# Chunked attention with two feed-forward layers: a new opening and other tiles for four split jobs

## The chip, the cores and the metric

The program runs on one core of one Trainium2 chip. The metric is the device time of one execution in microseconds (us).

## The reference

Attention over chunks of 32 queries, each with 8 memory keys and the 56 keys around the chunk, then two feed-forward layers over 3072 tokens. All is float32.

```python
for c in range(nc):                                    # 24 chunks, (B, H, S, D) = (4, 8, 768, 64)
    k_full = np.concatenate([mem_k, k_ctx], axis=2)    # 8 + 16 + 32 + 8 keys
    scores = scale * np.matmul(q_c, k_full.transpose(0, 1, 3, 2))
    a = np.exp(scores - np.max(scores, axis=-1, keepdims=True))
    out[:, :, c_start:c_end] = np.matmul(a / (np.sum(a, axis=-1, keepdims=True) + 1e-09), v_full)
x = out.transpose(0, 2, 1, 3).reshape(B * S, H * D)    # 3072 x 512
h = x @ w_in                                           # layer 1: 512 -> 2048
x = (np.maximum(h, 0.0) + np.log1p(np.exp(-np.abs(h)))) @ w_out
h = x @ moe2_w_in                                      # layer 2
return (h - np.tanh(h)) @ moe2_w_out
```

## The kernel before

**Products.** Every operand of the layers is split into a rounded high part and a low rest, and each product is three products on TensorE (`mm3`: high·high, high·low, low·high). The weights arrive as 64-bit words, and ScalarE and VectorE turn them into the two parts (`split_w`).

**Layout of the work.** The tokens are 24 attention units of 128 and six blocks of 512 tokens. An **opening** computes units 0 to 3 (tokens of block 0), splits the sixteen weight pairs of layer 1 and runs layer 1 on block 0. A main loop runs layer 1 on blocks 1 to 3, with the other attention units and jobs of the next layer stepped in between by `tick`. Then come one layer-1 phase (`y_phase`) and, for three groups of 1024 tokens, layer 2 as `h_phase` and `y_phase`. From the fourth block on the layers use seven block products instead of eight (`PRODUCTS`), for which `job_x` makes sums and differences of the layer-1 result `y1d`, splits each of them and stores it as `x2d`.

**What sets the order.** On TensorE, VectorE, ScalarE and SyncE (SP) instructions stand in the order of the code, and an engine that waits holds up all that is behind. In the opening a list of tokens, `OPENING`, is that order. For an attention unit u: Su scores, mxu maximum, exu exponentials, mlu normalization, Tu transposes, pTu their copy, Vu product with the values, xhu and xlu high and low part. For a weight pair f: yf and sf rebuild it, hf and lf split it (yi0, si0, hi0, li0 and yo0, so0, ho0, lo0 for the two halves of pair 0). Hf is the first product of layer 1 (12 matmuls of 512 columns), c1f, c3f, c4f the softplus and its split, Yf the second product. Kf stores, Lu loads, Zn is n matmuls on zeros. `ON_ACT` names units whose exponentials and sums run on ScalarE in eight pieces, `ASSIST` weight pairs whose bits ScalarE prepares, `HOME` the PSUM banks. `ORDER` is the order of the first loads. A load of SP or ScalarE uses one of eight completion counters in turn, and waits until the load eight places before it has landed.

**Key halves.** Units 0 to 3 compute scores for two heads at once (L258): their keys lie in a tile with two blocks, of which one has heads on partitions 0 to 63 and zeros elsewhere, the other on 64 to 127 (`qk_load_apart`, L225: two loads of 64 partitions, one of the queries). Later units use one load (`qk_load`) and 64 products per head (L270).

**Output tiles.** `job_x` takes a fresh tile of pool "o" (four buffers) for each of seven products; `high` (L508) lets ScalarE write the high part, `low` (L512) lets VectorE write the rest and stores both one tick later. Pool "g" holds `gh` and `gl`, three buffers each, for the layers' own splits (`y_steps`, L676, from the end of `h_phase` on). The jobs of groups 1 and 2 start at ticks 159, 169, 214 and 224, inside `h_phase`.

Of the kernel before, what the change touches and what calls it, by code (L numbers as in the profile page):

```python
# [8 lines left out]
F32 = mybir.dt.float32  # L9
F32R = mybir.dt.float32r  # L10
# [12 lines left out]
P = 128  # L23
NCH = P // CHUNK
NPAIR = H // 2
# [9 lines left out]
N = 512  # L35
NB = NTOK // N
UB = N // P
# [8 lines left out]


OPENING = """
Z7 S0 mx0 S1 ex0 mx1 S2 ml0 ex1 mx2 T0 S3 pT0 ml1 ex2 V0 mx3 T1 pT1 ml2 xh0 V1 ex3 xl0 ml3 T2 xh1
yi0 pT2 xl1 yo0 si0 Z6 T3 pT3 V2 so0 y1 V3 hi0 xh2 li0 xh3 s1 y2 xl3 xl2 Z11 H0 h1 ho0 l1 S4 c10 s2  # L50
H1 K1 c30 lo0 h2 c40 K0 mx4 y3 Y0 c11 l2 c31 y4 c41 K2 s3 H2 ex4 y6 Y1 ml4 h3 c12 l3 T4 s6 H3 pT4 K3
c32 y5 S5 c42 s4 V4 Y2 L6 c13 c33 y7 c43 h4 s5 Y3 h6 l4 h5 l6 K4 y8 H4 l5 K6 s7 K5 H5 c14 c34 s8 h7
H6 c15 c44 h8 l7 y9 l8 K7 H7 c35 y11 c45 K8 s9 c16 c36 H8 c17 y10 s11 Y4 h9 s10 Y5 c37 l9 h10 h11
c47 K9 mx5 y13 H9 c46 l10 c18 y14 l11 K10 H10 c19 s14 xh4 K11 y12 y15 H11 c38 xl4 ex5 s12 Y6 c48 h12
ml5 Y7 c110 l12 s13 K12 T5 H12 pT5 c39 c310 c49 h13 c410 V5 l13 c112 c111 S6 L7 xh5 H13 K13 mx6 h14
l14 ex6 s15 H14 K14 Y8 ml6 h15 xl5 T6 c311 Y9 pT6 c411 l15 c113 K15 S7 H15 mx7 ex7 Y10 ml7 V6 c313
c413 Y11 xh6 L8 c312 xl6 c412 c114 T7 Y12 c115 c314 pT7 V7 Y13 xh7 L9 c315 c415 xl7 c414
"""
ORDER = "qk0 qk1 qk2 qk3 v0 v1 i0 v2 v3 o0 w1 w2 w3 qk4 v4 w4 w5 w6 w7 qk5 v5 w8 w9 w10 w11 w12 w13 w14 w15"
ON_ACT = (1, 2, 5, 6)  # L60
ASSIST = (2, 5, 8, 10)
HOME = dict(
    S0="Y10", T0="H0", V0="Y1", S1="Y11", T1="H0", V1="Y0",
    S2="Y00", T2="A1", V2="Y0", S3="A0", T3="Y00", V3="Y1",
)

TB = 2 * N
# [27 lines left out]
def attention_ffn_ffn(  # L95
# [10 lines left out]
    nc = tc.nc  # L106
# [3 lines left out]
    wpool = ctx.enter_context(tc.tile_pool(name="w", bufs=1))  # L110
    xpool = ctx.enter_context(tc.tile_pool(name="x", bufs=1))
    gpool = ctx.enter_context(tc.tile_pool(name="g", bufs=3))
    tpool = ctx.enter_context(tc.tile_pool(name="t", bufs=2))
    opool = ctx.enter_context(tc.tile_pool(name="o", bufs=4))
# [14 lines left out]
    x2d = [[dpool.tile([P, 2, 2, N], F32, name=f"x2d{b}{q}") for q in range(1, 8)] for b in range(NT)]  # L129
# [95 lines left out]
    def qk_load_apart(u, q, home):  # L225
        n = NPAIR * P
        k = wpool.tile([P, 2, NCH * NPAIR * KEYS], F32, name=home)
        for j in range(2):
            (nc.gpsimd if u % 2 else nc.vector).memset(k[64 * (1 - j) : 64 * (2 - j), j], 0.0)
        for j in range(2):  # L230
            r = slice(64 * j, 64 * j + 64)
            nc.sync.dma_start(out=k[r, j], in_=qk[u][r, n:])
        nc.sync.dma_start(out=q, in_=qk[u][:, :n])
        att[u] = dict(
            q=q.rearrange("p (a t) -> p a t", a=NPAIR),
            kk=k.rearrange("p j (c a k) -> p j c a k", c=NCH, a=NPAIR),
        )
# [262 lines left out]
    def job_x(b, e, second=False):  # L500
        raw = wpool.tile([P, 2, 2, N], F32, name="w6" if second else "w15")
        nc.sync.dma_start(out=raw, in_=y1d[b][e])
        for _ in range(LEAD):
            yield
        b11, b21, b12, b22 = raw[:, 0, 0], raw[:, 0, 1], raw[:, 1, 0], raw[:, 1, 1]
        o = {}

        def high(q, src):  # L508
            o[q] = opool.tile([P, 2, N], F32R, name="o"), src
            nc.scalar.copy(out=o[q][0][:, 0], in_=src)  # L510

        def low(q):  # L512
            t, src = o.pop(q)
            minus(t[:, 1], src, t[:, 0].bitcast(F32))
            defer(put, t, ((0, 2, x2d[b][q - 1][:, e]),))

        high(1, b11)
        high(2, b21)
        yield
        low(1)  # L520
        low(2)
        minus(b12, b12, b11)
        high(3, b22)
# [12 lines left out]
        yield
        low(7)
        high(4, b21)
        yield
        low(4)  # L540
# [77 lines left out]
    def minus(out, x, y):  # L618
        nc.vector.tensor_tensor(out=out, in0=x, in1=y, op=ALU.subtract)  # L619
# [134 lines left out]
    def defer(f, *args, more=0):  # L754
        late.append((now[0] + more, f, args))
# [45 lines left out]
    with tc.manual_schedule(engines={mybir.EngineType.PE}):  # L801
# [8 lines left out]
        )  # L810
        if True:
            raws = {}
            qs = wpool.tile([P, UB, NPAIR * P], F32, name="w8")
            vs = wpool.tile([P, 2, NCH, NPAIR, D], F32, name="w11")
            early_home = dict(i0=10, o0=9)
            for name in ORDER.split():
                kind, i = name.rstrip("0123456789"), int(name.lstrip("qkviow"))
                if kind == "w":
                    raws[str(i)] = load_w((w1i, w1o), i)[0]
                elif kind == "qk":  # L820
                    if i < UB:
                        qk_load_apart(i, qs[:, i], f"w{15 - i}")
                    else:
                        qk_load(i)
                elif kind == "v":
                    v_load(i, vs[:, i - 2] if 1 < i < UB else None)
                else:
                    raws[name] = load_half(w1i if kind == "i" else w1o, 0, early_home[name])
            first = wpool.tile([P, 2, 2, 512], F32R, name="w0")
            weights["slot", 0] = first  # L830
            opening = ExitStack()
            pool = opening.enter_context(
                tc.tile_pool(name="ps0", bufs=1, space=bass.MemoryType.PSUM)
            )
            ps_yy = [pool.tile([P, 2, 512], F32, name=f"ps_yy{e}") for e in range(2)]
            pairs = dict(A=ps_a, Y0=ps_yy[0], Y1=ps_yy[1])
            banks = {n + e: t[:, int(e)] for n, t in pairs.items() for e in "01"}
            banks.update(pairs, H0=ps_h[0])
            going = {}

            for token in OPENING.split():
                op = token[:2] if token[0] == "c" else token.rstrip("0123456789")
                i = int(token[len(op) :])
                home = banks[HOME.get(token, "A0" if op == "T" else "A")]
                if op == "L":
                    at_load(i)
                elif op == "K":
                    keep_w1(i)
                elif op == "Z":
                    for _ in range(i):  # L850
                        nc.tensor.matmul(
                            out=ps_h[1], lhsT=zeros[:, :P], rhs=zeros, start=True, stop=True
                        )
                elif op == "S":
                    s_mm(i, home)
                    going["sm", i] = softmax(i, i in ON_ACT)
                elif op == "T":
                    t_mm(i, home)
                elif op == "pT":
                    t_out(i)  # L860
                elif op == "V":
                    v_mm(i, home)
                    going["x", i] = x_out(i)
                elif op == "H":
                    going["c", i] = chain1((1, 0, i), ff_h(i, ps_h[i % 2], x_tile(0), i == 0), nc.scalar)
                elif op == "Y":
                    if i == 0:
                        opening.close()
                        pool = ctx.enter_context(
                            tc.tile_pool(name="psy", bufs=1, space=bass.MemoryType.PSUM)  # L870
                        )
                        ps_y.extend(pool.tile([P, 512], F32, name=f"ps_y{e}") for e in range(4))
                    ff_y1((1, 0, i), i)
                else:
                    if op == "y":
                        going["w", i] = split_w(raws[str(i)], i)
                    elif op[0] == "y":
                        k = "io".index(op[1])
                        going["w" + op[1], i] = split_w(raws[op[1] + "0"], 0, op[1], first[:, k : k + 1])
                    kind = {"mx": "sm", "ex": "sm", "ml": "sm", "xh": "x", "xl": "x"}.get(op)  # L880
                    kind = kind or ("c" if op[0] == "c" else "w" + op[1:])
                    next(going[kind, i], None)
# [39 lines left out]
        for n, (t, f) in enumerate(steps):  # L922
# [107 lines left out]
```

## Time and profile before

| | us |
|---|---|
| median of 3 runs | 1069.93 (1068.26 to 1070.21) |
| the profiled execution | 1067.08 |
| its span, first to last instruction | 1064.9 |
| TensorE busy in the span | 1044.2 (98%) |
| VectorE, ScalarE busy | 729.5 (69%), 568.0 (53%) |
| mean granted TensorE clock | 0.994 |

The profiled execution is a run of its own: 2.85 us below the median, 2.2 us of it outside the span. In the rows below PE is TensorE, PEld its weight load, DVE VectorE, ACT ScalarE, POOL GpSimd; a trailing q is that engine's sequencer. L370 is line 370 of the kernel before.

### The profile page before, as it was taken

Reading aid. Unit: us, or ns where it says so; the run is one execution under the profiler, and the core shown is the slowest. Engines: PE = TensorE matmul, PEld = TensorE weight load, DVE = VectorE, ACT = ScalarE, POOL = GpSimd, SP = SyncE. Lnnn points to the kernel's source line nnn. Section 1 sums busy time; section 2 is a strip of 40 time slices with the busy share of each in tenths; the row PEclk is TensorE's granted clock in tenths of the full one; section 3 lists DMA queues with packets and bytes.
Section 4 is the critical chain, followed back from the end, with each engine's and each line's share of the span. In section 5 each row is a group of like instructions: output and inputs, shape, how many; then the busy total and the mean of one; then the engine's idle time right before and its main releaser. Section 6 shows DMA issues by size and latency. Waiting matters only on the chain.

```text
span 1064.9 us, 18364 instructions
## 1 busy us (share of the span) xinstructions
PE 1044.2 (98%) x7334; PEld 856.6 (80%) x7336; DVE 729.5 (69%) x1132; ACT 568.0 (53%) x903; POOL 4.4 (0%) x10
## 2 busy tenths in 40 slices
PE   6999999999999999999999998999999999999998
PEld 3788788887888888888888877888878888888887
DVE  6899455755755657486677686777477878446876
ACT  4998554645555555344555554554445554344553
POOL 1000000000000000000000000000000000000000
PEclk8999999999999999999999999999999999999999
DMA  9999855857776986999987998778899788656651
GB/s 288 409 408 378 299 177 178 286 195 224 262 256 233 317 305 200 337 355 340 335 342 279 365 362 339 300 290 317 296 322 348 289 326 305 230 169 215 242 209 60
DMA packets 100180, 303.18 MB, mean 285 GB/s; under 512 B 7936, under 2 KB 55040, under 8 KB 82432
## 3 DMA queue, kind: packets, MB, share of 16 engines
q1 hardware_dynamic: 100096, 302.02, 78.8%
q8 instruction: 58, 0.95, 0.4%
q14 instruction: 26, 0.21, 0.1%
HBM read 211.29 MB, written 90.70 MB: 284 GB/s over the span
## 4 chain that ended last, share of the span: by engine, by line
PE 91%; DMA 5%; DVE 1%; ACT 1%; issue 0%; SPq 0%; ACTq 0%
PE ps_y L370 45%; PE ps_h L370 31%; PE ps_b L370 12%; DMA x2d<-o 2%; PE ps_a L343 2%; PE ps_a L270 1%; DMA w<-in_qk 1%; DMA w<-in_w1o 1%; PE ps_a L320 1%; DMA wod<-o 1%; DVE w L619 0%; ACT tanh L642 0%; ACT kept L610 0%; DVE o L184 0%; ACT o L510 0%
## 5 line engine op out<-in xcount | busy, mean ns | idle before, releaser
L370 PE MATMUL ps_h<-x,w 128*128 128x512 f32 x900 | 215.1, 390 | 0.0
L678 ACT CAST gh<-w 128x512 fp32r<-128x512 f32 x224 | 139.3, 623 | 140.1 <-DVE gl L619 120.0
L619 DVE TENSOR_TENSOR gl<-w,gh 128x512 fp32r<-128x512 f32 x224 | 154.7, 691 | 70.4 <-ACT gh L678 63.9
L370 PEld LDWEIGHTS ps_h<-x,w 128*128 128x128 f32 x900 | 168.6, 188 | 35.2
L370 PE MATMUL ps_y<-gh,w 128*128 128x512 f32 x512 | 172.8, 399 | 0.4 <-issue 0.4
L370 PEld LDWEIGHTS ps_y<-gh,w 128*128 128x128 f32 x512 | 96.1, 188 | 21.9 <-issue 0.8
L370 PE MATMUL ps_y<-gh,x 128*128 128x512 f32 x352 | 109.2, 389 | 0.0
L370 PE MATMUL ps_y<-gl,w 128*128 128x512 f32 x256 | 99.7, 389 | 0.0
L370 PE MATMUL ps_y<-w,x 128*128 128x512 f32 x402 | 94.5, 389 | 0.0
L370 PEld LDWEIGHTS ps_y<-w,x 128*128 128x128 f32 x402 | 75.5, 188 | 15.7
L409 DVE TENSOR_TENSOR gl<-t,gh 128x512 fp32r<-128x512 f32 x64 | 43.9, 688 | 59.6 <-ACT gh L405 59.2
L370 PEld LDWEIGHTS ps_y<-gh,x 128*128 128x128 f32 x352 | 66.1, 188 | 13.7
L642 ACT ACTIVATE tanh<-sum 128x512 f32<-128x512 f32 x72 | 45.3, 632 | 54.2 <-DVE sum L615 54.2
L393 ACT ACTIVATE t<-ps_h 128x512 f32<-128x512 f32 x64 | 38.0, 597 | 66.3 <-PE ps_h L370 66.0
L370 PE MATMUL ps_b<-gh,x 128*128 128x512 f32 x176 | 68.5, 389 | 0.0
L370 PE MATMUL ps_h<-gh,x 128*128 128x512 f32 x176 | 68.5, 389 | 0.0
L370 PE MATMUL ps_y<-gl,x 128*128 128x512 f32 x176 | 68.5, 389 | 0.0
L430 ACT CAST o<-c 128x1024 fp32r<-128x1024 f32 (+1 forms) x32 | 31.0, 969 | 70.2 <-DVE c L475 40.4
L619 DVE TENSOR_TENSOR w<-w 128x512 f32<-128x512 f32 x88 | 60.5, 688 | 6.6 <-ACT w L393 5.5
L370 PE MATMUL ps_b<-w,x 128*128 128x512 f32 x216 | 55.0, 390 | 2.7 <-ACT kept L610 2.7
L370 PEld LDWEIGHTS ps_y<-gl,w 128*128 128x128 f32 x256 | 48.2, 188 | 9.0
L370 PE MATMUL ps_y<-x,w 128*128 128x512 f32 x240 | 55.2, 389 | 0.0
(157 smaller groups left out, 1618.1 us busy)
## 6 DMA issues: line engine op xcount, KB each, us to landing
x<-wod SPq DMA_DIRECT2D x44, 1024.0 KB, 4.7
x2d<-o SPq DMA_DIRECT2D x42, 512.0 KB, 6.2
w<-x2d SPq DMA_DIRECT2D x21, 1024.0 KB, 6.8
x<-wid SPq DMA_DIRECT2D x21, 1024.0 KB, 6.1
wod<-o SPq DMA_DIRECT2D x32, 512.0 KB, 5.5
qk<-in_qk SPq DMA_DIRECT2D x20, 768.0 KB, 6.8
x<-wid SPq DMA_DIRECT2D x18, 768.0 KB, 6.7
ring<-wod SPq DMA_DIRECT2D x12, 1024.0 KB, 5.8
```

The costliest lines, as they stand in the source:

```text
L270: nc.tensor.matmul(out=ps[cc, j, KEYS * p : KEYS * (p + 1)], lhsT=a["q"][r, p, cc], rhs=a["k"][r, c, p, :], start=True, stop=True,)
L320: nc.tensor.transpose(ps[:, p * P : (p + 1) * P], a["sm"][:, p].rearrange("p j k -> p (j k)"), ident)
L343: nc.tensor.matmul(out=ps[h : h + 64, p % 2, 2 * P + t0 : 2 * P + t0 + CHUNK], lhsT=a["v"][r, c, p, :], rhs=a["pT"][r, p, CHUNK * c : CHUN ...
L370: nc.tensor.matmul(out=ps, lhsT=a, rhs=b, start=first and i == 0, stop=last and i == 2, skip_group_check=on,)
L393: nc.scalar.activation(out=out, in_=x, func=AF.Softplus)
L409: nc.vector.tensor_tensor(out=gl, in0=t, in1=gh.bitcast(F32), op=ALU.subtract)
L430: nc.scalar.copy(out=hi, in_=src)
L619: nc.vector.tensor_tensor(out=out, in0=x, in1=y, op=ALU.subtract)
L642: nc.scalar.activation(out=t, in_=h, func=AF.Tanh)
L678: nc.scalar.copy(out=gh, in_=src)
```

## The change

It changes five things. (1) Unit 0 is loaded in one piece and scored by 64 short products (`qk_load`, L270). (2) For units 1 to 3 the upper key half goes out on ScalarE's queue, the lower on SP's, and unit 1's queries on ScalarE's. (3) Their tiles move up by one (`w15` to `w13`). (4) `OPENING`, `ON_ACT`, `ASSIST` and `HOME` have new values. (5) In `job_x` products 2, 5 and 7 of groups 1 and 2 take two tiles of pool "g" and go out as two stores.

```diff
-Z7 S0 mx0 S1 ex0 mx1 S2 ml0 ex1 mx2 T0 S3 pT0 ml1 ex2 V0 mx3 T1 pT1 ml2 xh0 V1 ex3 xl0 ml3 T2 xh1
...
+Z7 S0 mx0 ex0 Z6 S1 mx1 S2 ml0 ex1 T0 mx2 S3 pT0 ml1 ex2 mx3 T1 V0 pT1 ml2 yi0 V1 ex3 si0 T2 xh0 ml3
...
-ON_ACT = (1, 2, 5, 6)
-ASSIST = (2, 5, 8, 10)
+ON_ACT = (0, 1, 3, 7)
+ASSIST = (2, 5, 7, 10)
...
-        for j in range(2):
+        for j, queue in enumerate((nc.sync, nc.scalar)):
             r = slice(64 * j, 64 * j + 64)
-            nc.sync.dma_start(out=k[r, j], in_=qk[u][r, n:])
-        nc.sync.dma_start(out=q, in_=qk[u][:, :n])
+            queue.dma_start(out=k[r, j], in_=qk[u][r, n:])
+        (nc.scalar if u == 1 else nc.sync).dma_start(out=q, in_=qk[u][:, :n])
...
         def high(q, src):
-            o[q] = opool.tile([P, 2, N], F32R, name="o"), src
-            nc.scalar.copy(out=o[q][0][:, 0], in_=src)
+            if b and q in (2, 5, 7):
+                h, l = (gpool.tile([P, N], F32R, name=n) for n in ("gh", "gl"))
+                stores = [(x2d[b][q - 1][:, e, s], t) for s, t in enumerate((h, l))]
+            else:
+                t = opool.tile([P, 2, N], F32R, name="o")
+                h, l = t[:, 0], t[:, 1]
+                stores = [(x2d[b][q - 1][:, e], t)]
+            o[q] = h, l, src, stores
+            nc.scalar.copy(out=h, in_=src)
 
         def low(q):
-            t, src = o.pop(q)
-            minus(t[:, 1], src, t[:, 0].bitcast(F32))
-            defer(put, t, ((0, 2, x2d[b][q - 1][:, e]),))
+            h, l, src, stores = o.pop(q)
+            minus(l, src, h.bitcast(F32))
+            for place, t in stores:
+                defer(nc.sync.dma_start, place, t.bitcast(F32))
...
-                    if i < UB:
-                        qk_load_apart(i, qs[:, i], f"w{15 - i}")
+                    if 0 < i < UB:
+                        qk_load_apart(i, qs[:, i - 1], f"w{16 - i}")
```

The first rows of SP's queue, as a piece of the difference (`w_153` and the like are key tiles, `w_151` the queries):

```order
+L220 DMA qk<-in_qk 128x1536
+L232 DMA w_155<-in_qk 64x1024
+L232 DMA w_161<-in_qk 64x1024
 L233 DMA w_151<-in_qk 128x512
-L232 DMA w_159<-in_qk 64x1024 x2
-L233 DMA w_151<-in_qk 128x512
-L232 DMA w_165<-in_qk 64x1024 x2
-L233 DMA w_151<-in_qk 128x512
-L232 DMA w_171<-in_qk 64x1024 x2
+L232 DMA w_167<-in_qk 64x1024
 L233 DMA w_151<-in_qk 128x512
```

SP issues six loads before the first value load where it issued twelve; the four others now stand on ScalarE, behind its first table load and ahead of the first exponentials.

VectorE at the end of the opening's attention, before (`w_240` is weight pair 0, `w_187` and `w_566` pair 1, `c_538` the prepared bits of pair 2):

```order
L193 TENSOR_TENSOR w_240<-o,w_240 128x512
L180 TENSOR_SCALAR o<-o 128x1024
L184 SCALAR_TENSOR_TENSOR o<-w_187,o 128x1024 x2
L360 TENSOR_TENSOR x_395<-ps_yy_245,x_395 128x2x2x128
L360 TENSOR_TENSOR x_395<-ps_yy_244,x_395 128x2x2x128
L193 TENSOR_TENSOR w_566<-o,w_566 128x2x512
L173 SCALAR_TENSOR_TENSOR o<-o,c_538 128x1024
```

The same place now (`w_236` pair 0, `w_183` and `w_597` pair 1, `c_566` the bits of pair 2):

```order
L180 TENSOR_SCALAR o<-o 128x1024
L184 SCALAR_TENSOR_TENSOR o<-w_183,o 128x1024 x2
L193 TENSOR_TENSOR w_236<-o,w_236 128x512
L360 TENSOR_TENSOR x_462<-ps_yy_241,x_462 128x2x2x128
L360 TENSOR_TENSOR x_462<-ps_a,x_462 128x2x2x128
L173 SCALAR_TENSOR_TENSOR o<-o,c_566 128x1024
L193 TENSOR_TENSOR w_597<-o,w_597 128x2x512
```

The rebuild of pair 1 (s1) has moved ahead of the low part of pair 0 (li0), and the step s2 of pair 2 ahead of the low part l1.

SP's queue in the second job of group 1, as it stands now (before, each `x2d` tile went out as one store of 128x1024):

```order
L770 DMA x2d_100<-o 128x1024
L770 DMA x2d_101<-gh 128x512
L770 DMA x2d_101<-gl 128x512
L770 DMA x2d_102<-o 128x1024
L770 DMA x2d_104<-gh 128x512
L770 DMA x2d_104<-gl 128x512
L601 DMA x_4789<-wid_123 128x1536
L601 DMA ring<-wod_125 128x2048
L770 DMA x2d_105<-o 128x1024
L770 DMA x2d_106<-gh 128x512
L770 DMA x2d_106<-gl 128x512
L770 DMA x2d_103<-o 128x1024
```

Seven stores have become ten; the two weight refills (L601) keep their place between products 5 and 6.

## Rows read from the trace of the kernel before

**Rows 1.** Waits of TensorE: engine, line, releaser, us in total, times, longest

```profile
PE ps_yy L258 <- DMA w<-in_qk: 6.9, 3, 2.9
PE ps_b L370 <- ACT kept L610: 3.3, 2, 2.7
...
PE ps_y L370 <- ACT kept L610: 1.4, 1, 1.4
```

**Rows 2.** Busy time by window: length, busy us (count), granted clock, DMA share, GB/s

```profile
5.00:15.00 10.00, 3.76 (x70) 2.90 (x73) 3.98 (x8) 1.30 (x6) 0.20 (x1) 0.64 1.04 236
17.00:28.00 11.00, 7.62 (x209) 5.62 (x209) 9.51 (x21) 7.23 (x25) 0.00 (x0) 0.96 1.03 407
28.00:32.00 4.00, 3.67 (x119) 3.16 (x113) 2.23 (x4) 2.96 (x5) 0.00 (x0) 0.57 1.03 414
...
40.00:90.00 50.00, 50.00 (x343) 41.30 (x342) 49.02 (x58) 48.21 (x69) 0.00 (x0) 1.00 1.03 409
...
14.30:36.80 22.50, 18.06 (x363) 13.29 (x365) 17.70 (x33) 17.46 (x50) 0.00 (x0) 0.84 1.03 398
```

**Rows 3.** The chain that ended last, from 0 to 140: start, us, what

```profile
17.19 11.77 DMA w<-in_w1o
...
29.04 1.14 ACT o L165
```

**Rows 4.** Timeline of the opening: start, us, engine, instruction, count, idle before and releaser

```profile
1.20 3.17 PE L851 MATMUL ps_h<-gl 128*128 128x512 bf16 x7 [1.20 <-DVE gl L543]
...
2.65 1.10 SPq L232 DMA_DIRECT2D w<-in_qk  x2
...
7.31 1.60 PE L258 MATMUL ps_yy<-w,w 128*32 128x128 f32 x32 [2.95 <-DMA w<-in_qk]
...
13.33 0.69 DVE L295 TENSOR_REDUCE t<-ps_yy 128x8 f32<-128x512 f32 x1 [2.70 <-PE ps_yy L258]
...
14.33 0.31 ACT L304 ACTIVATE x<-ps_yy,t 128x64 f32<-128x64 f32 x1 [3.03 <-DVE t L297]
...
16.57 0.24 ACT L304 ACTIVATION_READ_ACCUMULATOR x<-ps_yy,t 128x1 f32 x1
...
31.11 2.58 PE L851 MATMUL ps_h<-gl 128*128 128x512 bf16 x10 [0.33 <-issue]
...
31.32 0.68 DVE L180 TENSOR_SCALAR o<-o 128x1024 uint32<-128x1024 uint32 x1
...
32.04 2.49 DVE L184 SCALAR_TENSOR_TENSOR o<-w,o 128x1024 uint32<-128x1024 uint32 x2
...
34.44 1.28 DVE L360 TENSOR_TENSOR x<-ps_yy,x 128x512 fp32r<-128x512 f32 x2
...
36.30 1.23 DVE L193 TENSOR_TENSOR w<-o,w 128x1024 fp32r<-128x1024 f32 x1 [0.57 <-ACT w L191]
...
37.44 1.22 DVE L173 SCALAR_TENSOR_TENSOR o<-o,c 128x1024 uint32<-128x1024 uint32 x1
...
37.69 2.56 PE L370 MATMUL ps_h<-x,w 128*128 128x512 f32 x10
```

**Rows 5.** Timeline of the second job of group 1, same columns

```profile
657.58 0.62 ACT L510 CAST o<-w 128x512 fp32r<-128x512 f32 x1 [5.77 <-DMA x2d<-o]
...
660.75 5.92 SPq L439 DMA_DIRECT2D x2d<-o  x3
...
664.93 1.65 PE L370 MATMUL ps_b<-w,x 128*128 128x512 f32 x6 [2.70 <-ACT kept L610]
...
678.48 0.61 ACT L678 CAST gh<-w 128x512 fp32r<-128x512 f32 x1
```

**Rows 6.** Stores of `x2d`: who waited for them (us, times), and their landing

```profile
  ACT o L510: 15.1, 5
...
DMA to landing us min/median/max: 2.6/6.8/11.1
```

**Rows 7.** Waits of SP's queue, as in group 1

```profile
SPq L593 <- PE ps_y L370: 166.5, 46, 9.1
```

More of the change, by code (lines that the diff above doesn't have):

```diff
@@ L48 @@
 OPENING = """
-Z7 S0 mx0 S1 ex0 mx1 S2 ml0 ex1 mx2 T0 S3 pT0 ml1 ex2 V0 mx3 T1 pT1 ml2 xh0 V1 ex3 xl0 ml3 T2 xh1
[L50 to L57, printed above, removed]
+Z7 S0 mx0 ex0 Z6 S1 mx1 S2 ml0 ex1 T0 mx2 S3 pT0 ml1 ex2 mx3 T1 V0 pT1 ml2 yi0 V1 ex3 si0 T2 xh0 ml3
+hi0 xh1 xl0 yo0 Z10 T3 pT2 so0 pT3 V2 y1 V3 xl1 ho0 s1 xh2 xh3 y2 li0 xl3 xl2 Z13 H0 h1 s2 y3 l1 S4
+h2 lo0 H1 c10 l2 s3 c30 H2 c11 c31 y4 c40 h3 c41 Y0 c12 l3 c32 y5 s4 H3 h4 s5 Y1 c13 l4 h5 y6 l5 H4
+y7 s6 H5 c42 mx4 c14 c33 Y2 h6 c43 c15 l6 y8 s7 H6 c34 c35 s8 ex4 Y3 h7 y12 l7 y9 c45 H7 ml4 y11 h8
+c44 s9 T4 c16 Y4 c36 pT4 c17 l8 V4 h9 c46 H8 y10 L6 l9 s11 H9 c18 c37 s10 K1 y14 S5 c47 h10 Y5 s12
+K0 h11 c19 K2 Y6 l10 h12 K3 xh4 mx5 y13 H10 l11 ex5 K4 xl4 c39 ml5 K5 H11 c38 y15 c48 K6 l12 c110 T5
+Y7 s13 K7 H12 c49 h13 s14 c310 pT5 V5 S6 L7 l13 h14 Y8 c111 l14 xh5 xl5 c410 H13 c311 mx6 K8 c112
+c411 s15 H14 c113 K9 ex6 Y9 K10 ml6 K11 T6 c312 Y10 pT6 h15 l15 K12 S7 V6 mx7 H15 xh6 L8 c313 ex7
+c413 xl6 c412 Y11 K13 c115 ml7 T7 K14 Y12 pT7 c114 V7 Y13 xh7 L9 c315 xl7 c314 c414 c415 K15
 """
 ORDER = "qk0 qk1 qk2 qk3 v0 v1 i0 v2 v3 o0 w1 w2 w3 qk4 v4 w4 w5 w6 w7 qk5 v5 w8 w9 w10 w11 w12 w13 w14 w15"
-ON_ACT = (1, 2, 5, 6)
-ASSIST = (2, 5, 8, 10)
+ON_ACT = (0, 1, 3, 7)
+ASSIST = (2, 5, 7, 10)
 HOME = dict(
-    S0="Y10", T0="H0", V0="Y1", S1="Y11", T1="H0", V1="Y0",
-    S2="Y00", T2="A1", V2="Y0", S3="A0", T3="Y00", V3="Y1",
+    S0="A", T0="Y00", V0="Y1", S1="Y10", T1="Y00", V1="Y0",
+    S2="A1", T2="H0", V2="A", S3="A0", T3="Y11", V3="Y1",
 )
@@ L812, in attention_ffn_ffn @@
             raws = {}
-            qs = wpool.tile([P, UB, NPAIR * P], F32, name="w8")
+            qs = wpool.tile([P, UB - 1, NPAIR * P], F32, name="w8")
             vs = wpool.tile([P, 2, NCH, NPAIR, D], F32, name="w11")
```

## The prediction

> **What bounds the kernel now.** I read the busy times first: TensorE works in 98% of the span at a mean granted clock of 0.994, so only 20.7 us of 1064.9 can be won without taking work from it. The waits of TensorE say where they lie. In the opening it waits 6.9 us for the queries and keys of the first units. Much later it waits three times, 3.3 + 1.4 = 4.7 us in all, for a copy (`kept`) that ScalarE makes of a finished PSUM bank [rows 1]. Both halves of the change aim at these two places.
>
> The windows show what the first place hangs on. From 5 to 15 us the DMA engines are as busy as ever (share 1.04), but move 236 GB/s; from 17 us on, with loads over all 128 partitions, 407 [rows 2]. In the slow stretch each unit moves 786 KB in 3.33 us. If its queries (262 KB, 128 partitions) go at 407, that is 0.64 us, and the two halves (524 KB) take 2.69 us: **195 GB/s for loads of 64 partitions**.
>
> The chain of waits gives the rest: a load of weights, which stands behind those of the keys on SP and lands 11.77 us after its issue, at 28.96, then ScalarE's first step on weight pair 1 at 29.04 [rows 3]. In the timeline I follow that pair: H1 starts at 37.69, as soon as the low part l1 is made (36.30 + 1.23 = 37.53) [rows 4]. From 40 to 90 us TensorE is busy all the time [rows 2]. So the opening is worth what H1 moves, if TensorE isn't starved behind it.
>
> **Loads.** Unit 0 now comes in one load over all partitions: its halves cost 524 KB at 407, 1.29 us, not 2.69; saved 1.4. For units 1 to 3 the lower halves stand on SP's queue and the upper on ScalarE's, so that both can be under way at once. The trace has no such pair. Bounds: they still take turns at 195 GB/s (1573 KB in 8.07 us, nothing won), or together reach 407 (3.86 us, 4.2 won). I take 300, midway, because on one queue lower and upper stood back to back too and showed no overlap: 5.24 us, 2.8 won. The weights of pair 1 then land 4.2 us earlier, at 24.8 (bounds 1.4 and 5.6: 27.6 and 23.4).
>
> Here a rule speaks against the change. The row says only that 64 partitions go at half the rate. The Trainium skill (DMA: Bandwidth & Descriptors, Rules for kernel authors) says of two transfers to disjoint partition halves "Don't bother": both use the same 16 engines and serialize, from two queues as from one. By it the landing would be the 27.6 above. The same skill (SBUF — State Buffer, the section on the DMA port swizzle) has 64 consecutive partitions reach half of 16 ports, which the half rate agrees with, and by which two halves side by side could use all. [...]
>
> ScalarE pays four issues behind its table load, 2.2 us if they take the 0.55 that SP needs for each half [rows 4]; its first exponentials come after 8 us, so this costs nothing; without that cover it would cost the 2.2. What stands behind these issues there is only ex0. Two memsets of 64x1024 leave VectorE, which is busy 4.0 of 10 us there [rows 2]: nothing.
>
> **From landing to H1.** Now 28.96 to 37.53 is 8.57. In the new order VectorE does s1, li0, xl3, xl2, s2, l1 in a row after ScalarE's 1.14: 1.14 + (0.68 + 2.49) + 0.64 + 1.28 + 1.22 + 1.23 = 8.68 (li0 taken as one of the two alike in 1.28) [rows 3, 4]. With the landing at 24.8, l1 is done at 33.5.
>
> **The other chain.** l1 needs h1 on ScalarE, which has its own queue from ex0 on. S0 waits for its load until 7.31; 1.4 us less makes 5.9 (bounds 4.4, where the zero products ahead of it end, and 7.3 if ScalarE's loads take the engines away). S0 took 1.60, from maximum to first exponential is 1.0, with unit 0's memset 1.2: ex0 starts at 8.7. From the first exponential of unit 1 to h1 and ho0, 14.3 to 36.8, ScalarE now works 17.46 us and waits 5.0 [rows 2]. In the new order the same stretch has three units in eight pieces rather than two; one takes 14.33 to 16.81, 2.48 [rows 4]. So 19.9 us of work. Of waits I can work out one: S1 stands behind six zero products of 0.45 (seven took 3.17), so ex1 can start at 7.5 + 2.7 + 1.6 + 1.0 = 12.8, 1.6 after ex0 ends. The old stretch had 5.0. Between 1.6 and 5.0 I take 4.5, near the old, since most of what ScalarE waited for there is still in the list. 8.7 + 19.9 + 4.5 + 1.23 = **34.3 for l1**, against 37.53. This chain, not the landing, is the later of the two, so a better landing alone wins little more. Worth 3.2.
>
> Behind H1 the order is H1, H2, Y0 instead of H1, Y0, H2; softplus needs its table load and gl comes behind s3 on VectorE, close to Y0's start. VectorE and ScalarE have 1.0 and 1.8 us to spare in 50 [rows 2], and ON_ACT and ASSIST keep four names each, so their work is as long as before. I take 0.3 back. **Opening: 2.9 us less** (bounds: 0, and 5.4 with the landing at 23.4 and l1 at 32.1).
>
> **The split jobs.** In the second job of group 1 ScalarE stands 5.77 us before a high part at 657.58, because the next of four "o" tiles is still being stored; all that is behind it, the `kept` copies too, comes late, and TensorE waits 2.70 us at 664.93 [rows 5]. Over all jobs line L510 waits 15.1 us in five places for such stores, which land 6.8 us after issue, at most 11.1 [rows 6]. With products 2, 5 and 7 elsewhere, a job needs four "o" tiles and has four, and three `gh` and `gl` and has three: none waits for a store of its own job. The three waits of TensorE for `kept` all lie behind such waits of L510, so 4.7 us goes; I take 4.5, for a first tile may still meet the store of the job before. It costs twelve more issues on SP, off the path.
>
> **Sum.** −2.9 − 4.5 = **−7.4**. The profiled execution would go from 1067.08 to 1059.7. The median of the runs shown is 2.85 higher than that execution; from it, 1069.93 − 7.4 = **1062.5**.
>
> **Rivals.** About 0.2% (2.1 us) is what a measurement of this kernel can tell from no change.
> - *The halves still take turns.* For it: the back-to-back loads of now. Landing 27.6, l1 at 27.6 + 8.68 = 36.3, 1.2 won, less 0.3: opening −0.9, in all −5.4, **1064.5**. This is what the rule quoted above comes to.
> - *The opening is given back.* Either VectorE and ScalarE, full from 40 to 90, can't follow an earlier TensorE, or the clock is low at the wrong time: from 28 to 32 the grant was 0.57, seven zero products took 3.17 at the low level and ten 2.58 in 31.11 to 33.7 [rows 2, 4], so thirteen before H0 could take 2.6 more. Opening about 0, in all −4.5, **1065.4**.
> - *The job waits only move.* The ten stores of a job share the eight counters of SP, refills stand between them, and ScalarE waits elsewhere. Against it: L510's waits are for tiles, and there are enough now. −2.9 alone, **1067.0**.
> - *More.* Halves at full rate and some 2 us less of waits on ScalarE, l1 at 32.4: 5.1 − 0.3 = 4.8, and all 4.7 of the jobs: **1060.4**.
> - *Slower.* `y_steps` takes its third `gh` at 678.48, the very buffer from which product 7 of the second job is stored; the last three stores go out from 660.75 to 666.67, so they land by 677.8 at worst [rows 5, 6]. If a refill that waits for TensorE stood before that store for the 9.1 us that the longest such wait took [rows 7], it would land at 686.9, and the layer's first products would wait 8.4 us: +8.4 − 7.4, **1070.9**. It decides from a store that goes out after 667.4 on; without the waits of now it goes out earlier.
> - *Nothing that counts:* an opening of −0.9 and jobs whose waits only move, **1069.0**.
>
> **Chances.** Forecast 0.45, more 0.11, halves in turn 0.15, opening given back 0.12, waits only move 0.08, slower 0.05, nothing 0.04. The forecast's own range is 1061 to 1064.3. For 8 in 10 the range takes in both sides of it, the halves and the opening given back, and the case of more with a baseline 1 us nearer to the profiled execution: **1059.5 to 1067**. Faster by over 0.2% (below 1067.8) are all but the last two; as these are worked out from one execution, I say 0.86, within 0.2% 0.09, slower 0.05.
>
> **What would show it.** Windows near 400 GB/s between 4 and 10 us: the halves overlap; near 240: they don't. S0 at 5.9, the second load of pair 1 landed at 24.8, l1 done at 34.3, no idle of TensorE from there to 130. No wait of L510 for `x2d`, none of TensorE for `kept`. I am wrong if TensorE waits anew between H1 and H8, if H0 starts at the low clock, or if `gh` in `y_steps` waits for a store.

## The result and the profile after

| | before | after |
|---|---|---|
| median, first measurement (us) | 1069.99 (1066.74 to 1071.82, 6 runs) | 1059.52 (1059.19 to 1060.25, 6 runs) |
| ratio | | 0.9907 (95%: 0.9892 to 0.9922) |
| the same pair, a later measurement | 1068.42 (1067.05 to 1070.22, 9 runs) | 1059.52 (1059.22 to 1059.92, 4 runs), 0.9916 (0.9903 to 0.9930) |
| profiled execution | 1067.08 | 1059.62 |
| its span | 1064.9 | 1057.8 |
| mean granted clock | 0.994 | 0.998 |

The changed kernel is faster by 10.5 us in the first measurement and 8.9 in the second. The profiled executions differ by 7.46, of which 0.35 lies outside the span. The runs of before scatter over 5 us; those of after lie within 1.1.

Waits of TensorE in the changed kernel, as in [rows 1] (lines have moved by eight from L510 on):

```profile
PE ps_a L258 <- DMA w<-in_qk: 1.7, 1, 1.7
PE ps_a L270 <- DMA qk<-in_qk: 1.5, 1, 1.5
...
PE ps_a L320 <- DVE sm L315: 1.1, 1, 1.1
```

The three waits for `kept` are gone. A wait for a softmax (L315) is new. The windows that answer to [rows 2]:

```profile
5.00:15.00 10.00, 6.58 (x134) 4.03 (x134) 2.86 (x8) 4.78 (x32) 0.19 (x1) 0.90 1.04 250
...
17.00:28.00 11.00, 9.81 (x312) 7.30 (x308) 9.43 (x20) 8.79 (x27) 0.00 (x0) 1.00 1.02 405
28.00:32.00 4.00, 4.00 (x19) 2.16 (x17) 3.93 (x6) 4.00 (x6) 0.00 (x0) 1.00 1.03 411
...
40.00:90.00 50.00, 50.00 (x342) 40.75 (x342) 47.82 (x58) 45.76 (x53) 0.00 (x0) 1.00 0.99 383
```

With two queues the slow stretch moves 250 GB/s; the prediction had taken 300 for the halves alone, and the rows show no such overlap. From 28 to 32 the clock is now full. The chain that ended last, to answer [rows 3]:

```profile
1.98 9.84 DMA w<-in_qk
...
11.84 7.92 DMA w<-in_w1i
...
27.73 2.91 PE ps_h L859 x13
30.64 2.08 PE ps_h L382 x8
```

It runs no longer through the last load of pair 1, but through the first weights, ScalarE's exponentials and the value products to H0. The timeline, to answer [rows 4]; the last row is unit 7's transpose:

```profile
5.85 1.18 PE L270 MATMUL ps_a<-qk 64*32 64x64 f32 x64 [1.48 <-DMA qk<-in_qk]
...
26.43 1.19 ACT L165 ACTIVATE o<-w 128x1024 f32<-128x1024 f32 x1 [0.50 <-DMA w<-in_w1o]
...
31.99 0.68 DVE L360 TENSOR_TENSOR x<-ps_a,x 128x512 fp32r<-128x512 f32 x1
...
32.72 0.76 PEld L382 LDWEIGHTS ps_h<-x,w 128*128 128x128 f32 x4 [0.44 <-DVE x L360]
...
33.93 3.02 DVE L193 TENSOR_TENSOR w<-o,w 128x1024 fp32r<-128x1024 f32 x3
...
34.64 1.53 PE L370 MATMUL ps_h<-x,w 128*128 128x512 f32 x5
...
117.98 0.63 PE L320 MATMUL ps_a<-ident,sm 128*128 128x128 f32 x4 [1.11 <-DVE sm L315]
```

The reader sees S0 at 5.85, the first step on pair 1 at 26.43 and H1 at 34.64. H1 does not follow l1 (done at 33.93 + 1.23 = 35.16, after H1 has begun), but the last third of H0, which waits for xl2 (31.99). No row shows a wait for `x2d` or for the third `gh` of `y_steps`; that is the first row here, the second is the landing of the stores ([rows 5, 6]):

```profile
672.90 0.61 ACT L686 CAST gh<-w 128x512 fp32r<-128x512 f32 x1
...
DMA to landing us min/median/max: 2.6/7.6/11.1
```

To see where the time went I counted TensorE's layer products of 512 columns by their starts, H1's first being number 0. All kernels have 4260 of them, in the same sequence of stages. Times are us, and each row is one execution:

| kernel | first step on pair 1 | H1 | H1 to no. 800 | 800 to 1800 | 1800 to last |
|---|---|---|---|---|---|
| before | 29.04 | 37.69 | 207.81 | 252.40 | 563.04 |
| after | 26.43 | 34.64 | 209.95 | 251.72 | 557.37 |
| after, measured again | 26.24 | 34.42 | 210.10 | 252.08 | 557.37 |
| e1, new jobs only | 27.00 | 35.67 | 211.46 | 251.92 | 557.37 |
| e2, new opening only | 26.26 | 34.44 | 210.48 | 251.76 | 564.87 |
| e4, old, halved stores | 28.02 | 36.88 | 209.16 | 251.79 | 564.92 |
| e6, old loads, new order | 30.26 | 38.43 | 209.59 | 251.72 | 557.37 |
| e3, one queue | 27.04 | 37.72 | 209.89 | 251.78 | 557.37 |
| e11, e3 with more zeros | 26.97 | 35.61 | 209.21 | 252.96 | 557.37 |
| e7, unit 6 on ScalarE | 27.21 | 35.40 | 210.37 | 251.72 | 557.37 |
| e9, unit 7's transposes later | 27.10 | 35.29 | 210.52 | 251.72 | 557.37 |
| e5, whole units | 26.75 | 34.95 | 209.52 | 251.72 | 557.37 |
| e8, e5 with other banks | 25.50 | 33.66 | 209.54 | 251.87 | 557.37 |
| e10, e8 with fewer zeros | 25.22 | 33.47 | 209.43 | 252.28 | 557.37 |

For before against after the columns give −3.05, +2.14, −0.68 and −5.67, in all −7.26. The −0.68 is not the change's: e1 and e4, with the old opening, need 251.92 and 251.79 there. The last column is the sharpest fact of the study: 557.37 in every kernel with the new job tiles, 563.0 to 564.9 in every one without.

### The profile page after: what moved, and what is told of

The parts are those of the page before. It is cut to its first block, busy times and chain, and to the rows that moved or that the text cites. A ratio compares the mean times of both kernels' runs of the same rounds, so it can differ in the third digit from the quotient of the medians.

```text
span 1057.8 us, 18468 instructions
## 1 busy us (share of the span) xinstructions
PE 1045.9 (99%) x7380; PEld 856.0 (81%) x7380; DVE 727.9 (69%) x1130; ACT 566.0 (54%) x901; POOL 4.4 (0%) x10
## 3 DMA queue, kind: packets, MB, share of 16 engines
q10 hardware_dynamic: 384, 1.05, 0.4%
## 4 chain that ended last, share of the span: by engine, by line
PE 95%; DMA 2%; ACT 1%; DVE 1%; issue 0%; ACTq 0%; DVEq 0%
PE ps_y L370 46%; PE ps_h L370 31%; PE ps_b L370 13%; PE ps_a L343 2%; PE ps_a L270 1%; DMA w<-in_qk 1%; PE ps_a L320 1%; DMA w<-in_w1i 1%; DMA y1d<-o 0%; PE ps_h L382 0%; PE ps_h L859 0%; ACT sm L304 0%; ACT x L304 0%; ACT x L358 0%; DVE st L295 0%; DVE c L495 0%
## 5 line engine op out<-in xcount | busy, mean ns | idle before, releaser
L627 DVE TENSOR_TENSOR gl<-w,gh 128x512 fp32r<-128x512 f32 x236 | 162.8, 691 | 70.4 <-ACT gh L686 64.0
```

## The experiments

In the expectations T1, T2 and so on name theories, and the verdicts below use these names. T3 and T7 are also the transposes of units 3 and 7 in `OPENING`; outside the expectations and the orders these are called transposes here.

**The two halves of the change apart.** e1 takes the kernel before with edit 5 alone.

```diff
+            if b and q in (2, 5, 7):
+                h, l = (gpool.tile([P, N], F32R, name=n) for n in ("gh", "gl"))
+                stores = [(x2d[b][q - 1][:, e, s], t) for s, t in enumerate((h, l))]
```

> The kernel before with edit 5 alone (products 2, 5 and 7 of groups 1 and 2 in tiles of pool g). Theory T1: the waits for x2d stores cost 4.7 us of TensorE and about 0.9 us around them in the profiled execution, and, because they depend on when a store lands, they are also what makes the runs of the kernel before scatter over 5 us. Then no wait of ScalarE for x2d is left, the runs lie within 1.5 us of each other, and the median goes down by 5.6 plus most of the 2.9 by which the median lay over the profiled execution: some 8 us, ratio about 0.9925. Rival T2: the scatter comes from elsewhere (the opening, the chip); then the median goes down by 4.7 to 5.7 only, ratio 0.995, and the spread stays at 4 to 5 us.

Measured: 1060.97 (1059.7 to 1062.9) against 1067.81, ratio 0.9943 (0.9926 to 0.9959), no wait for `x2d`. The gain of 6.8 lies between the two theories, and the spread of 3.2 us too. The jobs are worth 5.7 or more, but the opening scatters as well: e1's profiled execution shows how, in a wait for unit 7's load and the windows around it.

```profile
109.05 1.05 PE L270 MATMUL ps_a<-qk 64*32 64x64 f32 x64 [2.15 <-DMA qk<-in_qk]
```

```profile
106.00:109.00 3.00, 0.90 (x4) 0.40 (x3) 0.29 (x1) 2.10 (x3) 0.00 (x0) 1.00 0.96 360
109.00:113.00 4.00, 3.95 (x71) 3.20 (x72) 2.07 (x3) 1.14 (x2) 0.00 (x0) 0.57 1.08 412
```

Behind the wait the granted clock is 0.57 for four microseconds of full work: 0.43 × 4 = 1.7 us more. Without these two, 211.46 − 2.15 − 1.7 = 207.6, as in the kernel before.

e2 is the changed kernel with `high` and `low` of `job_x` as they were.

```diff
-            if b and q in (2, 5, 7):
...
+            o[q] = opool.tile([P, 2, N], F32R, name="o"), src
```

> The changed kernel with the tiles of job_x as they were (edits 1 to 4 alone). Theory T1: H1 is 3.05 us earlier, but only 0.9 to 1.6 us of it is left at 250 us, because units 5 to 7 and the blocks behind them wait anew; the runs scatter as those of the kernel before. Ratio 0.9985, spread 4 to 5 us, TensorE waits for kept again. Rival T3: the opening keeps its 3.05, which in the changed kernel was masked by the jobs: ratio 0.997. Rival T2 (scatter from the opening): the spread falls to about 1 us and the median gains 3 to 4 us.

Measured: 1067.26 (1064.36 to 1069.75, 12 runs), ratio 0.9995 (0.9981 to 1.0008). As T1 said; the waits for `kept` are back (2.8 and 1.5), and the spread with them. T3 and T2 fall: alone the new opening shows no gain that this measurement can tell.

e4 keeps the old tiles and halves the stores.

```diff
-            defer(put, t, ((0, 2, x2d[b][q - 1][:, e]),))
+            if b and q in (2, 5, 7):
+                for s in range(2):
+                    defer(nc.sync.dma_start, x2d[b][q - 1][:, e, s], t[:, s].bitcast(F32))
```

> The kernel before with its o tiles in job_x, but products 2, 5 and 7 of groups 1 and 2 go out as two stores of 128x512 each, as in the change. Theory T1 (a job is short of tiles): ScalarE still waits for x2d in four or five places for about 15 us, and the time is that of the kernel before within 0.2%. Rival T5 (what mattered is the size of the stores, a smaller one lands sooner): the waits shrink by half or more and the time goes down by 3 us or more, ratio 0.997 or lower.

Measured: 1068.14 (1065.56 to 1070.0, 12 runs), ratio 1.0005 (0.9994 to 1.0015). Who waited for `x2d`, then the same wait as in [rows 5], both of e4:

```profile
  ACT o L510: 16.8, 5
```

```profile
657.32 0.62 ACT L510 CAST o<-w 128x512 fp32r<-128x512 f32 x1 [5.65 <-DMA x2d<-o]
```

T5 falls: the number of tiles counts, not the size of the stores. The windows behind the long wait for `kept`, of before, e2 and e4 in turn, show why a kernel with the old jobs doesn't always lose the same:

```profile
664.00:669.00 5.00, 4.07 (x18) 3.37 (x19) 4.81 (x8) 3.41 (x7) 0.00 (x0) 1.00 0.89 364
```

```profile
664.00:669.00 5.00, 5.00 (x16) 3.95 (x17) 3.73 (x7) 2.56 (x5) 0.00 (x0) 0.66 0.70 282
```

```profile
664.00:669.00 5.00, 4.33 (x13) 3.51 (x14) 4.55 (x8) 2.81 (x6) 0.00 (x0) 0.66 0.90 364
```

In the profiled execution of before the clock stayed full behind the wait; in the two others it was 0.66, 0.34 × 5 = 1.7 us more. That is most of 564.9 against 563.0.

**One queue or two.** e3 puts every first load back on SP.

```diff
-        for j, queue in enumerate((nc.sync, nc.scalar)):
+        for j, queue in enumerate((nc.sync, nc.sync)):
...
-        (nc.scalar if u == 1 else nc.sync).dma_start(out=q, in_=qk[u][:, :n])
+        nc.sync.dma_start(out=q, in_=qk[u][:, :n])
```

> The changed kernel with all first loads on SP's queue, upper halves and the queries of unit 1 too. Theory T1 (loads of 64 partitions on two queues share one rate, so nothing overlaps): the stretch from 5 to 15 us moves 240 to 260 GB/s as with two queues, the first step on weight pair 1 starts at 26.4 within 0.5, and the time is that of the changed kernel within 1 us (ratio 0.991). Rival T4 (two queues do help somewhat, which is why 26.4 is below the 27.6 worked out for halves in turn): that step starts at 27.6 or later, H1 is 1 us or more later than in the changed kernel, the time 0.5 to 1.2 us longer.

Measured: 1062.61 (1061.92 to 1063.76), ratio 0.9956 (0.9940 to 0.9973). The landing (27.04) lies between the two theories, and the time is 3.1 us above the changed kernel's, more than the 0.5 to 1.2 of T4. But the profile doesn't show a slower rate as the cause of so much. The slow stretch of e3, then of e1, both on one queue:

```profile
5.00:15.00 10.00, 6.23 (x134) 4.07 (x135) 2.86 (x8) 4.94 (x32) 0.19 (x1) 0.88 1.04 231
```

```profile
5.00:15.00 10.00, 5.53 (x96) 4.34 (x97) 5.01 (x11) 2.40 (x14) 0.19 (x1) 1.00 1.05 267
```

In six executions one queue gave 228 (e11) to 267 GB/s, in five two gave 235 (e9) to 262 (e2). Of the six only e3 and e11 have the loads of the changed kernel, and with 231 and 228 both lie below all five, so that some per cent for the second queue aren't excluded. But e7 and e9, with two queues, had their first step on pair 1 as late as e3 (27.21 and 27.10), with H1 at 35.40 and 35.29 and not 37.72. What is different is the wait of unit 3's transposes in e3 (0.85 in the changed kernel, 1.08 in e7), and the clock behind it, first e3, then e7:

```profile
25.32 0.66 PE L320 MATMUL ps_yy<-ident,x 128*128 128x128 f32 x4 [2.05 <-DVE x L360]
```

```profile
26.00:33.00 7.00, 6.60 (x136) 4.68 (x138) 6.68 (x9) 6.03 (x9) 0.00 (x0) 0.51 1.02 409
```

```profile
26.00:33.00 7.00, 6.38 (x147) 4.45 (x149) 6.39 (x9) 6.22 (x8) 0.00 (x0) 1.00 1.03 410
```

e11 fills e3's wait with zero products.

```diff
-hi0 xh1 xl0 yo0 Z10 T3 pT2 so0
+hi0 xh1 xl0 yo0 Z15 T3 pT2 so0
```

> The kernel with all first loads on SP's queue (1062.6), with fifteen instead of ten zero products ahead of T3. There pair 1 landed at 26.98, no later than in two profiled kernels with two queues (27.15 and 27.04, whose H1 started at 35.4 and 35.3), yet H1 started at 37.7: TensorE stood 2.05 us before T3 (0.85 in the changed kernel, 1.08 in the one with unit 6 on ScalarE), and from 26 to 33 us its granted clock was 0.51, so that twelve zero products and H0 took 3 us longer. Theory T1: what the second queue gave is not the rate but 0.6 us of landing, which decides whether TensorE stands long enough there to be given the low clock; five more zero products (1.2 us) fill the wait, the grant from 26 to 33 stays near 1, H1 starts at 35 to 35.6 and the time is 1060.0 to 1060.8. Rival T4: one queue is slower by itself: H1 at 37 or later whatever fills the wait, 1062 or more.

Measured: 1062.77 (1061.09 to 1065.44, 10 runs), ratio 0.9953 (0.9938 to 0.9968). In the profiled execution (1061.09) all of T1 is there but the time: unit 3's transposes wait 1.08, the granted clock is 1.00 from 26 to 33, H1 starts at 35.61. A wait of 1.05 before 301.63, for which the profile names nothing, is more than the 0.3 by which it misses T1's time. Five of the ten runs took 1061.1 to 1061.9, the others 1063.6 to 1065.4. So the clock explains H1 in the profiled executions, but the median of one queue isn't lowered by the five zero products, and what the slower half of the runs met is not in any trace: why one queue costs 3 us is **open**.

e6 has the new order and jobs on the loads of before (unit 0 in halves too, S0 in one bank).

```diff
-ON_ACT = (1, 2, 5, 6)
-ASSIST = (2, 5, 8, 10)
+ON_ACT = (0, 1, 3, 7)
+ASSIST = (2, 5, 7, 10)
```

> The kernel before with the new OPENING, ON_ACT, ASSIST and HOME and the new jobs, but the loads as they were: unit 0 in halves too, everything on SP's queue. With the kernel that has the new jobs alone (old order, old loads: 1061.0) and the changed kernel (new order, new loads) it tells the order from the loads. Theory T1: the new order starts its products earlier and meets the loads late, so that TensorE stands still longer before H0, gets the low clock there, and the order alone gains nothing: H1 at 37 to 39, the time 1061.0 to 1063.5, as with one queue (1062.6). Rival T10: the order is what wins (s1 ahead of li0, three units on ScalarE), the loads little: 1059.5 to 1060.3.

Measured: 1062.73 (1062.17 to 1063.92), ratio 0.9948 (0.9935 to 0.9960), H1 at 38.43: T1 in its numbers. Its reason holds in part: H0 ran at full clock, and the low clock (0.54 from 21 to 28 us) lay on the products ahead of unit 3's transposes. Their copy on ScalarE came late, and the first step on pair 1 behind it:

```profile
29.78 0.59 ACT L332 COPY x<-ps_yy 128x512 f32<-128x512 f32 x1 [3.06 <-PE ps_yy L320]
30.26 1.16 ACT L165 ACTIVATE o<-w 128x1024 f32<-128x1024 f32 x1
```

In the same measurement the changed kernel took 1059.52, so under the new order the new loads are worth 3.2 us. Against e1 (1060.97, ratio 0.9943) the new order on the old loads gains nothing; that it loses the 1.8 us between the medians isn't shown, since the runs overlap and the ratios agree. The changed kernel's median is 1.4 us below e1's, from different measurements and with runs that overlap too. The new loads under the old order weren't run.

**The changed kernel again.** An unchanged copy.

> The changed kernel itself once more, beside the others on one chip. The traces so far show three sources of scatter: the rate of the 64-partition loads between 3 and 14 us (235 to 271 GB/s, one queue or two), stretches of 3.4 us at half the granted clock, each worth 1.7 us where TensorE is busy, and the jobs. Theory T1: with the jobs' waits gone and H0 at full clock the changed kernel is steady whatever the chip, 1059.5 within 0.8, spread under 1.5 us, ratio 0.992 on a chip where the kernel before takes 1067.8. Rival T7: its lead of 10.5 us is a property of the program, and the chip shifts both: then 1057.3, ratio 0.9907.

Measured: 1059.52 (1059.22 to 1059.92), ratio 0.9916 (0.9903 to 0.9930). T1: it is the kernel before that varies, from one measurement to the next and from run to run.

**What is given back behind H1.** e7 lets unit 6 take unit 7's place on ScalarE.

```diff
-ON_ACT = (0, 1, 3, 7)
+ON_ACT = (0, 1, 3, 6)
```

> The changed kernel with unit 6 instead of unit 7 among those whose exponentials run on ScalarE in eight pieces. In the changed kernel the transposes of unit 7 wait 1.1 us at 118 us for its softmax. Theory T1: that wait is one place where the opening gives back what it won; it goes, nothing as long comes in its place, and the time is 0.7 to 1.1 us shorter than the changed kernel's. Rival T11: VectorE and ScalarE are full there, so the wait moves to unit 6 or to the next product: within 0.4 us of the changed kernel.

Measured: 1060.27 (1060.02 to 1061.03), ratio 0.9925 (0.9913 to 0.9938). T1 falls; transposes now wait at two places, 0.31 and 0.80 us. e9 gives unit 7's transposes more time instead.

```diff
-c413 xl6 c412 Y11 K13 c115 ml7 T7 K14 Y12 pT7 c114 V7 Y13 xh7 L9
+c413 xl6 c412 Y11 K13 c115 ml7 K14 Y12 T7 pT7 c114 Y13 V7 xh7 L9
```

> The changed kernel with T7 and V7 each moved behind the next Y (Y12 T7 pT7 c114 Y13 V7 instead of T7 K14 Y12 pT7 c114 V7 Y13): the softmax of unit 7 gets the 2.7 us of Y12 to finish. Moving the work to ScalarE or off it (unit 6 instead of 7) had only moved the wait. Theory T1: the 1.1 us wait of T7 at 118 us goes and nothing takes its place, 1058.3 to 1058.7 against 1059.5. Rival T13: V7, or the next product's softplus behind pT7 on ScalarE, waits instead: 1059.2 to 1060.

Measured: 1060.39 (1059.02 to 1062.59), ratio 0.9933 (0.9911 to 0.9956). T13: unit 7's transposes no longer wait, the next product does, for xh7 and then xl7:

```profile
125.28 0.50 PE L370 MATMUL ps_h<-x,w 128*128 128x512 f32 x1 [0.70 <-ACT x L358]
126.00 2.79 PE L370 MATMUL ps_h<-x,w 128*128 128x512 f32 x11 [0.22 <-DVE x L360]
```

From H1 to no. 800 both need 210.4 to 210.5 us, no less than the changed kernel.

**Whole units.** e5 loads units 1 to 3 as unit 0: one load each over 128 partitions, 64 short products, a pair of score banks for each.

```diff
+        t = wpool.tile([P, NPAIR * (P + NCH * KEYS)], F32, name=home)
+        nc.sync.dma_start(out=t, in_=qk[u])
...
+    S0="A", T0="H0", V0="Y1", S1="Y1", T1="H0", V1="Y0",
+    S2="A", T2="H0", V2="A", S3="Y0", T3="Y11", V3="Y1",
```

> The changed kernel, but units 1 to 3 too are loaded whole over 128 partitions and scored by 64 short products (no key halves, no memsets, all on SP's queue, score banks moved so that each unit has a pair). Theory T1: the half rate belongs to loads of 64 partitions and not to this place or to the queue; then 5 to 15 us moves 400 GB/s, 1573 KB of halves at 250 become the same keys in 786 KB at 400, and the first step on pair 1 starts 3.5 to 4.5 us earlier, at 22 to 23. H1 follows by at most 2.5, since ScalarE's chain then ends last, and of that about a third is left at 250 us, as in the change itself: 0.5 to 1 us faster than the changed kernel. Rival T8: what limits there is the load of unit 0 and the start of the queues; 250 GB/s remain and nothing changes. Rival T9: the opening gains at H1 as the landing does and keeps it: 2.5 to 4 us faster.

(The bytes stay the same; "in 786 KB" there is a slip.) Measured: 1059.61 (1059.39 to 1060.33), ratio 0.9918 (0.9904 to 0.9931). The slow stretch of e5:

```profile
5.00:15.00 10.00, 6.79 (x270) 4.76 (x271) 6.13 (x16) 5.85 (x34) 0.00 (x0) 0.83 1.02 418
```

T8 falls: the low rate belongs to loads of 64 partitions. T1 is right in the rate and wrong in the step and the time, and T9 falls too: nothing is won, because ScalarE stands before unit 3's exponentials (first row), so that the first step on pair 1 (last row) comes 4.5 us behind its landing; SP's issue at 22.22 is the one that waits for it.

```profile
21.03 0.32 ACT L297 ACTIVATE x<-ps_yy,t 128x64 f32<-128x64 f32 x1 [4.69 <-PE ps_yy L336]
...
22.22 0.33 SPq L147 DMA_DIRECT2D w<-in_w1o  x1
...
26.75 1.19 ACT L165 ACTIVATE o<-w 128x1024 f32<-128x1024 f32 x1
```

e8 gives unit 3 the bank pair that unit 1's value products don't use.

```diff
-    S2="A", T2="H0", V2="A", S3="Y0", T3="Y11", V3="Y1",
+    S2="Y0", T2="H0", V2="A", S3="A", T3="Y11", V3="Y1",
```

> The kernel with whole units, with the score banks of units 2 and 3 exchanged (unit 2 in Y0, unit 3 in A). With whole units pair 1 landed at about 22.2 (the load eight places behind it went out then), 4 us before that of the changed kernel, but H1 started at 34.95: ScalarE stood 4.69 us before the exponentials of unit 3, which share a bank pair with the value products of unit 1, and everything behind them, the first step of pair 1 too (26.75), came late. Theory T1 (with these loads ScalarE's chain ends last, not the landing): without that wait H1 starts at 31.5 to 32.5. What H1 wins is kept to the end where the order stays the same: from H1 to the 800th product of layer 1 the new order took 209.5 to 210.1 us with H1 anywhere from 34.4 to 38.4. So 2 to 3 us faster than the changed kernel, 1056.5 to 1057.5. Rival T12: before 34.4 VectorE and ScalarE can't follow, and TensorE waits between H1 and 140 us for what it won: 1059.0 to 1059.6. Rival T8: the wait only moves along ScalarE and H1 stays at 34 to 35: 1059.5.

Measured: 1058.99 (1058.48 to 1059.52), ratio 0.9920 (0.9899 to 0.9941). H1 at 33.66 misses T1's 31.5 to 32.5: the wait has in part moved, to unit 3's transposes, behind zero products at the low clock. What H1 does win is kept (209.54 to no. 800). e10 shortens those zeros.

```diff
-hi0 xh1 xl0 yo0 Z10 T3 pT2 so0
+hi0 xh1 xl0 yo0 Z4 T3 pT2 so0
```

> The kernel with whole units and exchanged banks (1059.0), with four instead of ten zero products ahead of T3. There the ten took 3.11 us at the low clock, T3 started only behind them at 24.38, and ScalarE stood 2.74 us before its copy, with the first step of pair 1 behind it (25.50, landed at 22.1). Theory T1 (the order on ScalarE and TensorE, not the landing, now holds H1): T3 at 22.3 to 22.8, that step at 23.3 to 24, H1 1.5 to 2 us earlier (31.7 to 32.2), kept to the end: 1057.0 to 1057.6. Rival T14: with fewer zero products TensorE stands more, the low clock stays on through H0, and H1 starts at 33.7 or later: 1059 to 1061. Rival T12: H1 is early, but given back before 140 us: 1059.

Measured: 1058.28 (1057.69 to 1059.01), ratio 0.9915 (0.9899 to 0.9931). Unit 3's transposes come at 23.64 and H1 at 33.47, 0.2 earlier where 1.5 to 2 were expected: unit 1's value products stand 2.0 us before 19.39 for nothing that the profile names, and four zero products at half clock take 1.91.

```profile
19.39 1.71 PE L336 MATMUL ps_yy<-x,v 64*64 64x32 f32 x55 [2.02 <-issue]
21.94 1.91 PE L851 MATMUL ps_h<-gl 128*128 128x512 bf16 x4
```

T1 is wrong in size, T14 and T12 in the time. It is the fastest kernel of the study; its runs don't overlap those of the changed kernel, but 1.2 us is less than the comparison with before can tell.

## Why the prediction was right, step by step

The total for the profiled executions was −7.4 and came out −7.46. That is luck: two steps of it were off and cancelled, the opening by 2 us too much and the jobs by 1.2 too little, and 1.0 of the −7.46 lies where the sum had no term (0.68 between nos. 800 and 1800, 0.35 outside the span).

**The median failed in its baseline.** It was forecast at 1062.5 and came out at 1059.52, outside the forecast's own range (1061 to 1064.3) and only just inside the wide one (from 1059.5). The number is nearest to the rival *more* (1060.4), but not by its reasons: the halves didn't reach full rate, and l1 came at 35.16, not at 32.4. The step that failed took 7.4 off the median of before, as if the 2.85 us by which it lay over its profiled execution stayed. The changed kernel has no such gap (1059.52 against 1059.62).

**Split jobs, −4.5: the mechanism was right, the size too small.** No wait for `x2d`, none for `kept`, and −5.67; e1 shows it for this edit alone, with the same 557.37. [Rows 1] give 4.7 of idle time; from product start to product start the three gaps are 1.00, 3.08 and 1.78 where 0.23 passes without a wait, 5.2 too much in all, and the product behind each comes 0.1 late too. What I didn't see is the clock behind them: 563.04 in one execution with old tiles, 564.9 in the two others. With 1.8 us more in some runs the median of before lies above its profiled execution. That the other runs lost it at this place is argued from e2 and e4, not seen. The rivals "waits only move" and "slower" fall: the third `gh` is taken at 672.90 without a wait.

**Loads: the step "I take 300" failed.** Two queues moved 250 GB/s where one moved 236 in the kernel before, and one queue moved 228 to 267 in other executions. So the halves share one rate, but for some per cent at most (231 and 228 against 235 to 262 with the same loads). This is the rival *the halves still take turns*. It is also the rule of the Trainium skill (DMA: Bandwidth & Descriptors, Rules for kernel authors), with which these rates agree. I read the other page too narrowly: from its ports I had both halves use all, but the Trainium skill (SBUF — State Buffer, "Can I just issue two DMAs to hit both halves?") answers no, with 6% measured. 250 against 236 is 6% too, though the scatter of one queue alone is larger. What whole loads would give is seen in e5: 418.

**Landing 24.8:** 26.43, between forecast and rival (27.6). A fixed number for it was the wrong form: the same opening code had it at 29.04 in before, 28.02 in e4 and 27.00 in e1. The profiled execution of before was a late one.

**From landing to l1, 8.68:** measured 35.16 − 26.43 = 8.73. **S0 at 5.9:** 5.85, but e7 and e9 waited 2.6 and 3.0 us for the same load instead of 1.5. **l1 at 34.3:** 35.16. And l1 wasn't what H1 waits for: that is xl2, through H0. It was so in the kernel before too, where I took l1 for it and the last third of H0 waited for xl2:

```profile
35.78 1.20 PE L382 MATMUL ps_h<-x,w 128*128 128x512 f32 x4 [0.24 <-DVE x L360]
```

With s1 ahead of li0, from the first step on pair 1 to the end of xl2 it takes 6.24 instead of 6.68. So H1's 3.05 consists of 2.61 from the landing and 0.44 from the order, and part of the 2.61 is that the execution of before was a late one: against e1 H1 wins only 1.03.

**"I take 0.3 back" failed.** From H1 to no. 800 the new order needs 209.2 to 210.5 in every kernel, in e6 too, where H1 starts later than in before. The old one needs 207.6 to 207.8: 207.81 in before, 207.6 in e1 without its wait, and in e4, whose clock is low from 36 to 40 us (0.57, 1.7 us, 1.4 of them behind H1), 209.16 − 1.4 = 207.8. Some 2 us of the 3 that H1 wins are the price of the new order behind it. From product start to product start the wait of unit 7's transposes is 1.2 of the 2.14, two starts at 142.6 and 143.0 us come 0.4 later than without a wait, and three just behind H1 0.3; the last 0.2 are open. The wait at 142.6 is again one for a tile that is still being stored, now on VectorE, whose copy the product waits for:

```profile
141.90 0.69 DVE L423 COPY o<-ps_y 128x512 f32<-128x512 f32 x1 [3.02 <-DMA y1d<-o]
142.64 0.19 PEld L370 LDWEIGHTS ps_y<-gh,w 128*128 128x128 f32 x1 [0.53 <-DVE o L423]
```

e7 left 0.80 of the 1.1 in its place and 0.31 at unit 6, and e9 moved the wait to the next product; [rows 2] and the same window after show VectorE busy for 49.02 and 47.82 of 50 us before that place. The rival *the opening is given back* holds for two thirds of the opening in size, but for neither of its reasons: the clock isn't low at H0 (1.00 from 28 to 32), and e6 pays as much without an earlier H1.

**−2.9 for the opening** is −0.9 by no. 800, the size of the rival *the halves still take turns*. The median of the runs also gained by steadiness, which the sum had no term for: runs with the new opening and the old jobs (e2) spread over 5.4 us, with the new jobs and the old opening (e1) over 3.2, with both over 1.1.

## What to carry to other kernels

When a tile is short, count the waits behind the engine that takes it, and expect TensorE to lose more than the idle time shown, since a wait there may be followed by a few microseconds at half clock; taking such a wait away also takes scatter out of the runs. Follow a product's start to a later fixed point before you call an earlier start a gain: here two thirds of it were gone 200 us later, and the new order without its loads gained none. A landing time or rate read from one execution carries a scatter that only more executions show.

## What the runs showed of the hardware

Waits of TensorE of 2.05 (e3), 2.15 (e1), 2.6 (e4) and 2.8 us (e2) were followed by a mean granted clock of 0.51 to 0.66 in the windows of 4 to 7 us shown behind them; one of 2.70 us in the kernel before [rows 5] was not (1.00). Units whose keys come in halves of 64 partitions, with queries over 128, moved 228 to 267 GB/s from 5 to 15 us whether on one queue or two, with the DMA engines at a share of 1.04 to 1.05; whole units over 128 partitions moved 418 at 1.02.
